# Batch 0 of an attention and SwiGLU kernel: running sums in 72-column segments, the causal mask by a product, single PSUM banks, and a new order of loads

## The chip, the cores and the metric

The kernel runs on one core of a Trainium2 chip. The time is the device time of one execution in microseconds (us). Every kernel was run several times, an experiment always beside runs of the kernel before on the same chip. The engines are called by the profile's names: PE (TensorE), DVE (VectorE), ACT (ScalarE), POOL (GpSimd), SP (SyncE); PEld is PE's weight load. The tiles in the profile's lines: rawk, rawq and rawv are the buffers in which loads land, ck and cq their bf16 casts, kq the transposed operands of the score product with the bias rows in them, HL and seg_rows the source of those rows, pt the exponentials, vt the cast V, ot the attention's output, XT its transpose, which the FFN reads, and wg, wv and wo the weights.

## The reference, cut to what matters

```python
# q, k, v: (8 batches, 8 heads, 576, 64)   s: (8, 8, 576)
cum = np.cumsum(np.maximum(s, 0.0), axis=-1)
bias = -(cum[:, :, :, None] - cum[:, :, None, :])
scores = np.where(causal, -1e9, q @ k.T / 8 + np.minimum(bias, 0.0))
attn = softmax(scores)                     # with the row maximum taken off
x = (attn @ v).transpose(0, 2, 1, 3).reshape(4608, 512)
g = x @ w_gate                             # w_gate, w_val: 512 x 1536
out = (g * sigmoid(g) * (x @ w_val)) @ w_out
```

The kernel brings the bias into the score product as extra rows of q and k: the running sum, split into a high and a low bf16 part, and constants.

## The kernel before

Batch 0's attention stands alone at the start. Then nine tiles of 512 tokens go through the feed-forward part (FFN), and the attention of the later batches is woven into them. The kernel fixes the order of each engine's instructions by the order of its Python calls. A "half batch" is four heads; half batches 0 and 1 are batch 0.

Loads of q, k and v go through SP's queue. There are three buffers for half batches, but one for V:

```python
def load_one(hb, name, rs=(0, NR)):          # "k" or "q" of one half batch
    ... loaded[name, hb] = raw.tile([...], tag="raw" + name)       # 3 buffers
    nc.sync.dma_start(...)
def load_v(b, cs):
    if 0 in cs:
        loaded["v", b] = raw.tile([...], tag="rawv", bufs=1)       # ONE buffer
    for c in cs:
        nc.sync.dma_start(t[0:n, c, :, :], v[b, ...])
```

The running sums, all 64 heads at once over 576 columns, then their rows by DMA into q and k:

```python
nc.vector.tensor_scalar(s_sb, s_sb, 0.0, 8.0, ALU.max, ALU.mult)
nc.vector.tensor_tensor_scan(c8, ones, s_sb, 0.0, ALU.mult, ALU.add)
nc.vector.tensor_copy(HL[:, 0, 1, :], c8)                           # high part
nc.vector.tensor_sub(HL[:, 1, 1, :], c8, HL[:, 0, 1, :])            # low part
nc.vector.tensor_copy(HL[:, 2:4, 0, :], HL[:, 0:2, 1, :])
```

Behind the last scores of batch 0 come the loads for what follows, and then the first FFN tile with "hooks" that run at given items (an item is roughly one gate or value product group):

```python
if h == 7:
    aug(3, SP4)                      # bias rows of half batch 3
    load_qk(3)
    load_v(1, range(5))
    load_qk(4)
    cast_one(2, "k", nc.gpsimd); cast_one(2, "q", nc.gpsimd)
    load_qk(5)
    w_load("o", 0); w_load("o", 1)
...
hook = {1: prep_one(2, 0), 2: prep_one(2, 1), 3: prep_one(2, 2), 4: prep_one(2, 3),
        6: cast_one(3, "k"), cast_one(3, "q")}                      # shortened
n0 = 6 if tt == 0 else 0             # item at which attention starts in the first tile
```

The load of V for batch 2 is not in this list. It is called from inside the attention code, when the third and fourth head of half batch 2 are scored.

The softmax here doesn't subtract the row's maximum and nothing guards it: scores larger than these inputs give would overflow.

## Time and profile before

| | kernel before |
|---|---|
| time, median of 3 runs | 381.24 us (380.64 to 382.00) |
| profiled span | 377.7 us |
| PE busy | 359.2 us, 95% of the span |
| first score product | 11.23 us |
| first gate product | 31.60 us |
| first gate product of the second tile | 79.38 us |
| last product | 373.29 us |

The prediction below shows most lines of this profile. Two views are added here, because they also belong here. The first is the order of work on SP from 50 to 66 us (start, length, queue, source line, what, count):

```profile
51.77 0.62 SPq L155 DMA_DIRECT2D rawk<-in_k_dram  x1
52.43 0.47 SPq L155 DMA_DIRECT2D rawq<-in_q_dram  x1
52.99 0.41 SPq L155 DMA_DIRECT2D rawk<-in_k_dram  x1
53.51 0.55 SPq L155 DMA_DIRECT2D rawq<-in_q_dram  x1
55.28 8.52 SPq L172 DMA_DIRECT2D rawv<-in_v_dram  x5
```

These are half batch 4, half batch 5, and then V of batch 2, in this order. (Before them, the five issues of V for batch 1 had held SP from 27.46 to 51.72 us, single ones for up to 7.31 us: half batches 4 and 5 stood behind V here too, but were still in time for their casts.) The second is one line of the order of work on ACT: the cast of half batch 5's k, with no idle time before it (a wait would stand in brackets at the end).

```profile
59.18 1.15 ACT L254 CAST ck<-rawk 128x1152 bf16<-128x1152 f32 x1
```

### The profile page before, as it was taken

What the parts mean: (1) busy time and instruction counts of PE and PEld (TensorE: products, weight loads), DVE (VectorE), ACT (ScalarE), POOL (GpSimd) and SP (SyncE); (2) the same over time, 40 slices, a digit from 0 to 9 for tenths busy, and PEclk for the clock granted to TensorE, in tenths of its full rate; (3) what the DMA queues carried; (4) which work ended last, traced back from release to release, by engine and by line L of the source; (5) the groups of instructions that cost most, each with busy time, mean ns of one, the idle gap of its engine ahead of it and who ended that gap; (6) DMA issues with size and microseconds to landing.
All of it is one profiled execution on the core that took longest, in us unless ns stands there. A gap on an engine that the chain in (4) does not pass through costs nothing.

```text
span 377.7 us, 8635 instructions
## 1 busy us (share of the span) xinstructions
PE 359.2 (95%) x3207; PEld 229.4 (61%) x3246; DVE 289.9 (77%) x577; ACT 242.7 (64%) x459; POOL 207.7 (55%) x326
## 2 busy tenths in 40 slices
PE   3679999999999999999999999999999999999996
PEld 3566556655555556865586558655875575466465
DVE  7766787457895899769975998589958876975984
ACT  8686788677976877578766875697365523323321
POOL 7784357445374646595559556875675426214320
PEclk9899999999999999999999999999999999999999
DMA  7999999988487998499659765998223133001103
GB/s 243 198 250 263 198 254 272 343 252 177 162 179 247 232 282 219 104 252 309 160 163 286 197 161 164 238 189 162 51 74 109 26 26 128 0 2 69 43 2 111
DMA packets 100729, 64.22 MB, mean 170 GB/s; under 512 B 81888, under 2 KB 85824, under 8 KB 100688
## 3 DMA queue, kind: packets, MB, share of 16 engines
q1 hardware_dynamic: 91248, 46.15, 51.5%
q0 software_dynamic: 9440, 17.53, 18.2%
q8 instruction: 25, 0.41, 0.5%
q14 instruction: 16, 0.13, 0.1%
HBM read 37.90 MB, written 19.86 MB: 153 GB/s over the span
## 4 chain that ended last, share of the span: by engine, by line
PE 85%; DVE 6%; DMA 5%; ACT 2%; issue 1%; DVEq 0%; ACTq 0%; SPq 0%
PE bank L626 22%; PE bank L641 22%; PE bank L711 17%; PE bank L375 9%; PE bank L413 6%; PE bank L670 5%; DMA pk<-ks 2%; PE wide L375 2%; DVE pp L633 1%; ACT pt L388 1%; DVE kq L326 1%; DVE ht L649 1%; PE one L413 1%; DMA kq<-HL 1%; DMA s_sb<-in_s_dram 1%
## 5 line engine op out<-in xcount | busy, mean ns | idle before, releaser
L388 ACT ACTIVATE pt<-bank 128x512 bf16<-128x512 f32 x224 | 106.7, 506 | 26.2 <-PE bank L375 17.9
L626 PE MATMUL bank<-XT,wg 128*128 128x512 bf16 x420 | 109.7, 379 | 1.2 <-DVE pp L633 0.2
L641 PE MATMUL bank<-XT,wv 128*128 128x512 bf16 x411 | 109.3, 379 | 1.1
L631 ACT ACTIVATE th<-bank 128x512 bf16<-128x512 f32 x108 | 64.7, 599 | 58.8 <-PE bank L626 53.5
L633 DVE SCALAR_TENSOR_TENSOR pp<-th,bank 128x512 bf16<-128x512 bf16 x108 | 73.7, 683 | 23.8 <-ACT th L631 23.2
L649 DVE SCALAR_TENSOR_TENSOR ht<-pp,bank 128x512 bf16<-128x512 bf16 x108 | 74.1, 687 | 10.4
L658 POOL TENSOR_TENSOR ht<-ht 128x512 bf16<-128x512 bf16 x35 | 40.5, 1156 | 52.9 <-DVE su L656 52.8
L375 PE MATMUL bank<-kq 128*128 128x128 bf16 (+4 forms) x504 | 67.5, 240 | 0.3 <-DVE ht L649 0.2
L375 PEld LDWEIGHTS <-kq 128*128 128x128 bf16 x576 | 46.2, 98 | 33.8 <-issue 5.1
L641 PEld LDWEIGHTS <-wv 128*128 128x128 bf16 x432 | 38.3, 98 | 35.3
L626 PEld LDWEIGHTS <-wg 128*128 128x128 bf16 x432 | 38.4, 98 | 35.0 <-issue 1.1
L391 POOL TENSOR_SCALAR_AFFINE_SELECT pt<-pt 128x512 bf16<-128x512 bf16 x64 | 41.5, 648 | 30.9 <-ACT pt L388 30.4
L413 PEld LDWEIGHTS <-pt 128*128 128x128 bf16 x960 | 41.0, 98 | 16.6 <-issue 0.7
L413 PE MATMUL bank<-vt,pt 128*128 128x65 bf16 x840 | 41.8, 194 | 0.5 <-DVE ot L430 0.5
L447 POOL DMA_DIRECT2D xs<-ot x24 | 21.8, 908 | 28.0 <-DVE ot L430 28.0
L711 PEld LDWEIGHTS <-ht 128*128 128x128 bf16 x336 | 31.2, 98 | 4.3
L197 POOL DMA_DIRECT2D kq<-HL x52 | 32.7, 632 | 0.1
L430 DVE TENSOR_TENSOR ot<-bank,rc 128x320 bf16<-128x320 f32 x56 | 27.5, 492 | 1.9
L396 POOL TENSOR_SCALAR_AFFINE_SELECT pt<-pt 128x64 bf16<-128x64 bf16 x64 | 17.4, 272 | 18.5 <-ACT pt L388 18.3
L711 PEld LDWEIGHTS <-su 128*128 128x128 bf16 x252 | 23.6, 98 | 3.3
L670 PE MATMUL bank<-wo,ht 128*128 128x512 bf16 x90 | 24.2, 379 | 0.3
L776 POOL TENSOR_TENSOR ysb<-ysb 128x512 f32<-128x512 f32 x12 | 15.3, 1272 | 15.3 <-DVE ysb L770 15.3
(96 smaller groups left out, 395.6 us busy)
## 6 DMA issues: line engine op xcount, KB each, us to landing
rawk<-in_k_dram SPq DMA_DIRECT2D x15, 576.0 KB
rawq<-in_q_dram SPq DMA_DIRECT2D x15, 576.0 KB
rawv<-in_v_dram SPq DMA_DIRECT2D x32, 256.0 KB
out_dram<-ysb POOLq DMA_DIRECT2D x32, 256.0 KB, 3.8
xs<-ot POOLq DMA_DIRECT2D x24, 160.0 KB, 4.0
ks<-ck SPq DMA_DIRECT2D x11, 288.0 KB
qs<-cq SPq DMA_DIRECT2D x11, 288.0 KB
wg<-in_moe_w_gate_dram POOLq DMA_DIRECT2D x2, 768.0 KB, 11.8
```

What stands on the lines that cost most here:

```text
L375: nc.tensor.matmul(sc[:, o : o + w], T[:, 1, e * S + 128 * tj : e * S + 128 * (tj + 1)], T[:, 0, e * S + lo : e * S + hi], start=True, sto ...
L388: nc.scalar.activation(pt[:, c0 : c0 + W], sc[:, 0:W], AF.Exp, scale=0.125)
L391: nc.gpsimd.affine_select(pt[:, 1088:1600], pt[:, 1088:1600], pattern=[[0, 4], [1, 128]], compare_op=ALU.is_ge, fill=zreg, base=0, channel ...
L413: nc.tensor.matmul(av[:, bi * (D + 1) : (bi + 1) * (D + 1)], pt[:, c0 : c0 + 128], VT[b % 2][:, tj, h, :], start=(tj == 0), stop=(tj == bi),)
L626: nc.tensor.matmul(pg, WG[j][:, c, f0 : f0 + 128], xt[:, c, :], start=(c == 0), stop=(c == 3),)
L631: nc.scalar.activation(th, pg, AF.Tanh, scale=0.5)
L633: nc.vector.scalar_tensor_tensor(pp, in0=th, scalar=1.0, in1=pg, op0=ALU.add, op1=ALU.mult)
L641: nc.tensor.matmul(pv, WV[j][:, c, f0 : f0 + 128], xt[:, c, :], start=(c == 0), stop=(c == 3),)
L649: nc.vector.scalar_tensor_tensor(hp[:, 2 * k2 : 2 * k2 + 2, :].rearrange("p a n -> p (a n)"), in0=pp, scalar=0.5, in1=pv, op0=ALU.mult, op ...
L658: (nc.vector if ft == NFT - 1 else nc.gpsimd).tensor_sub(hp[:, 1:3, :], hp[:, 1:4:2, :], hp[:, 0:3:2, :])
L670: nc.tensor.matmul(py, hps[ft // 2][:, 2 * (ft % 2) + half, c0 : c0 + 128], WO[ft // WKO][:, ft % WKO, :], start=(ft == 0), stop=(ft == NF ...
L711: nc.tensor.matmul(ps, lhs(p), rhs(p), start=(first and p == 0), stop=(last and p == NP - 1), skip_group_check=True,)
```

## The change

Its intent is to start the scores of batch 0 earlier, keep PE and ACT busier until the FFN begins, and spread the loads. Core of the diff, with cuts:

```diff
+    seg_c, seg_s, seg_tri, seg_rows, lower = ...        # small tiles; pt buffers 8 -> 7
-    2 two-bank tiles and 4 one-bank tiles in PSUM, regrouped after batch 0
+    8 one-bank tiles throughout
 # running sums of batch 0 on (8 heads x 8 segments) x 72
+    nc.vector.tensor_scalar(seg_s, ...); nc.vector.tensor_tensor_scan(seg_c, ...)
+    nc.tensor.matmul(bank[0:64, 0:1], seg_tri, seg_c[:, SEG - 1 : SEG])   # sums of earlier segments
+    nc.vector.tensor_add(seg_s, seg_c, bank...); high and low part into seg_rows
+    aug_first(0, 0)                                     # 4 row DMAs on SP; 12 more later
     nc.vector: maximum, scan and high part of the other batches (576 columns), now behind these
 # mask (batch 0 only)
-    POOL affine_select on the exponentials
+    matmul(sc, ident, lower, start=True, stop=False)    # adds -32768 above the diagonal
 # queues
-    load_qk(1) at the very start; V, half batches 2 and 3 on SP
+    load_qk(1) on SP behind aug_first(0, 0); V(0), weights, half batches 2 and 3 on POOL's queue
 # end of batch 0
+    values(0, 1) behind scores(5), values(2, 3) behind scores(6), the rest behind scores(7)
+    six gate products of 2 column blocks on the 3 head pairs that are ready, ahead of the last transposes
 # first FFN tile
-    the lists shown above; n0 = 6; prep of half batch 3 at steps (0,3) (1,3) (2,1) (2,3)
+    at_item(4 and 5, cast_one, 2, ...); at_item(5, init_vt, 1); at_item(6, load_v, 1)
+    at_item(6 to 9, prep_one, 2, ...); at_item(14, cast_one, 3, ...)
+    at_item(14, w_load, "o", 0); at_item(15, load_qk, 4); at_item(16, w_load, "o", 1)
+    at_item(20, load_qk, 5)
+    n0 = 10; prep of half batch 3 at steps (1,3) (2,1) (2,3) (3,1)
```

## The prediction

> **What bounds the kernel now.** I read the page first (engine shares, then the 40 slices), then the busy time by stretches, then the chain of waits of the first 36 us, then the order of work on each engine up to 60 us. The page says PE is busy for 359.2 of 377.7 us, so the question is only where the missing 18.5 us lie. The stretches (columns: start and end, length, busy time and count of PE, PEld, DVE, ACT, POOL, then granted clock, DMA share, GB/s) answer it:
>
> ```profile
> 12.00:13.00 1.00, 0.14 (x3) 0.04 (x1) 0.64 (x1) 1.00 (x2) 0.09 (x2) 0.90 0.71 164
> 14.00:15.00 1.00, 1.00 (x11) 0.96 (x10) 0.00 (x0) 1.00 (x2) 0.00 (x0) 0.50 1.28 229
> 22.00:23.00 1.00, 0.28 (x3) 0.18 (x2) 0.00 (x0) 1.00 (x2) 1.00 (x3) 1.00 1.17 223
> 28.00:29.00 1.00, 1.00 (x29) 0.86 (x27) 0.82 (x4) 0.72 (x2) 1.00 (x2) 1.00 1.17 214
> ...
> 31.60:40.00 8.40, 8.29 (x56) 4.59 (x59) 6.34 (x9) 5.66 (x10) 2.30 (x2) 1.00 1.13 253
> 40.00:50.00 10.00, 9.43 (x71) 5.38 (x71) 7.84 (x13) 8.80 (x19) 2.39 (x5) 1.00 1.21 199
> 160.00:200.00 40.00, 39.79 (x379) 26.56 (x382) 31.82 (x68) 29.43 (x59) 26.74 (x41) 1.00 0.89 222
> ```
>
> Until 11 us PE waits for data, from 12 to 23 us it idles behind ACT, from 23 us it is full. From 31.6 us (the first gate product) to 377.7 us it is busy 339.3 of 346.1 us, and of the 6.8 us missing 3.75 lie after 320 us. So nearly all that this change can win lies before 31.6 us, and nothing in it shortens the 346 us after that. The chain of waits (start, length, what) shows what sets the 31.6 us:
>
> ```profile
> 0.81 2.93 DMA s_sb<-in_s_dram
> ...
> 4.35 1.36 DVE c L237
> ...
> 7.94 3.24 DMA kq<-HL
> ...
> 11.88 1.03 ACT pt L388
> ...
> 14.44 1.91 PE one L297 x18
> ...
> 24.00 0.92 PE one L413 x30
> 24.91 0.80 PE wide L375 x9
> 25.71 1.36 PE one L413 x45
> ...
> 30.91 0.65 ACT XT L468
> 31.56 0.04 issue
> 31.60 0.38 PE bank L626
> ```
>
> Three pieces: s, its scan and split, and the bias rows' DMA, up to 11.2 us; sixteen exponentials that end at 26.96 us; then values, transposes and a wait for the last copy into XT, 4.64 us more. ACT runs one head in 1.675 us once steady, from the order of work on ACT:
>
> ```profile
> 20.26 6.70 ACT L388 ACTIVATE pt<-wide 128x1024 bf16<-128x1024 f32 x8
> ```
>
> 13.3 us for eight heads, plus the two gaps ACT has before it (0.56 us at 14.0 and 1.27 us at 16.83), is the 15.1 us of this stage.
>
> **What the Trainium skill says.** "ScalarE: Activation LUTs", What ACT_TABLE_LOAD costs: an ACTIVATE with immediates takes 186 ns + 0.833 ns a column, back-to-back ones overlap by about 93 ns. That gives 1039 ns for 1024 columns; this trace has 1024. Splitting a head's two exponentials into four should then cost some 0.1 to 0.2 us a head; the trace, where later heads already run as four, has four of them in 1.69 us, so almost nothing. "TensorE: Matmul & The Clock Gate", Part 1: an idle PE drops to half clock and needs about 3.4 us of work to come back. The trace agrees: clock 0.50 from 13 to 16 us after the wait at 10 to 11, and the 18 transposes there take 1.91 us, 106 ns each; later ones take some 72 ns (five in 0.36 us). "VectorE: DVE Perf Modes", Zero memsets can be issued as uint32: a memset takes one cycle per element whatever its type. The trace is a little better, 1.07 us for 1216 columns, so about 0.56 us for 608. "DMA: Bandwidth & Descriptors", Issuing engines are not separate DMA queues: moving loads to another queue only saves issue time, the engines are shared. The DMA share of 1.0 to 1.3 from 13 us on agrees that order, not queue, matters.
>
> **The change part by part.**
>
> Running sums by segments. The scan over 576 columns (1.35 us), the casts (0.83, 0.75, 0.45 us) leave the head of the chain. In their place, on 64x72: maximum, scan, a one-column product over the segments, add, cast, difference. I estimate 0.25, 0.25, 0.45, 0.25, 0.15, 0.2 us and 0.2 for handovers, from the 0.19 us of the 128x5 reciprocal and an eighth of the long ones: 1.75 us. DVE first has four new memsets of 608 columns, 4 x 0.59 from 1.0 us, to 3.4 us; s lands at about 3.6; the rows are ready at about 5.4 us instead of 7.85. Four row DMAs at 0.62 to 0.83 us of issue, the last landing 2.2 us later (the shortest of this kind): 10.0 us instead of 11.18. Taken alone that is 1.2 us won.
>
> But scores(0) also needs q's columns, which DVE copies from PSUM, and DVE's program order now has in front of them: the long maximum 0.55, the long scan 1.37, the HL cast 0.84 (for later batches), and three memsets 1.77 us. 5.4 + 4.53 = 9.9; two copies 1.5 (the trace has 1.44 and 1.46 a pair): 11.4 us. So the first product moves from 11.2 to about 11.4, the first exponential stays near 11.9. The wait on the row DMA becomes a wait on DVE.
>
> DVE stays behind: cast of q's second half 0.45, k's copies 1.5 and q's 1.5 (k's moved from ACT), cast of k of the second half batch 0.78: 15.7 us. PE's order puts that batch's k transposes before scores(2), so scores(2) starts at about 16.4 and ACT, done with two heads at 11.9 + 3.4 = 15.3, waits about 1.4 us. Before, ACT waited 0.56 + 1.27 = 1.83 us. Nothing won.
>
> Mask by a product. Per head it adds a 512- and a 64-column product to PE, 0.22 + 0.03 us (a 512-column product of the gate advances 0.86/4 = 0.215 us): 2.0 us for eight heads, and removes 0.63 + 0.24 us of POOL. The first five are free, since PE idles 0.76 to 0.86 us a head there; the last three cost up to 0.75 us, because from 23 us PE is full. The POOL selects were off the chain.
>
> Single banks. Four exponentials a head, 1.69 against 1.675 us: 0.1 us over eight heads. Gain: PE no longer waits for a two-bank tile, but seven banks less four held by transposes leave three, so it runs little ahead. I call it zero.
>
> Values earlier, gates on three pairs. After scores(5) values 0 and 1 (0.55 us a head: 15 products in 0.55 to 0.57), after scores(6) 2 and 3, after scores(7) the rest. With ACT at the end of head 5 at 11.9 + 6 x 1.69 + 1.6 = 23.6, PE ends scores(5) at some 22.2; values 1.1, scores(6) 1.05, values 1.1, scores(7) 1.05: 26.5; values 4, 5 1.1; transposes and values 6 (0.37 + 0.55 + 0.74), values 7 0.55: 29.8; six gate products 1.3 in the place of 14 warming products: 31.1; last transposes 0.4 and copy 0.7: 32.2. At that moment 1.3 us of the FFN is done, so the comparable start is 30.9 us against 31.6.
>
> Loads. V, weights and the next batches go by POOL's queue. In the kernel before, 17.2 us pass from 12.5 us (end of the quiet spell) to 29.7 us (value weights issued at 16.67 landed 13.0 us later), for V, two weight blocks and one half batch. The same sum of bytes now starts near 8.5 us, so they land near 26 to 27 us, before their use at 31. Hidden. In the first FFN tile attention starts four items later; ACT was busy 8.8 of 10 us at 40 to 50 and stays off the chain; of the 0.57 us PE lost there perhaps 0.3 is won.
>
> Sum: 0.7 + 0.3 = 1.0 us by this working, 380.2 us.
>
> **The rivals.** (1) DVE is quicker than I add up, and the rows' DMA decides after all: scores from 10.0 us, no wait at head 2. Then the whole stage is 1.4 + 1.4 us earlier and the gain is 3 to 4 us: 377 to 378. For it: the change is plainly aimed at this, and it fills PE with warming products to be ready; my small-operation times are estimates. Against: the DVE sum is made of measured durations. (2) Loads starve the FFN: V on POOL's queue costs POOL perhaps 1 us an issue (0.91 us for the 24 stores of ot), a gate block lands 10.0 to 13.7 us after issue here, so one that leaves at 15 to 18 us may land after 30 us. That would take back 1 to 3 us: 381 to 383. Against: POOL is freed of selects, and the DMA has 4 us more. (3) Bias rows of heads 2 to 7 come too late: twelve more small DMAs on SP in line behind q and k, 0.62 us each, landing 2.2 to 7.0 us later in this trace. Heads 2 and 4 have 1 us of slack or less, so 0 to 2 us lost.
>
> **Range and chances.** The working gives 380.2. The estimates that could move it mostly err towards a gain (rival 1, and PE at full clock in the transposes), so I take about 1 us more: 379.3 us. Low end, rival 1 in full and some of the first tile's gaps: 376.2. High end, rival 2 or 3 cancelling the tail's gain: 381.6. Faster by over 2% needs 373.6 us, 7.6 us less: the stage before 31.6 us would have to shrink by a quarter, chance 0.04. Slower by over 2% would need starving of 7.6 us, 0.02.
>
> **What would show each step.** Right: first score product at about 11.4 us with DVE's copy of q, not DMA, as its releaser; a gap on ACT of more than 1 us before head 2; four exponentials in 1.69 us; last exponential at 27 to 28 us; gate products among the last values; the first value product at about 32 us; clock near 1.0 from 10 us on. Wrong: scores at 10 us released by the row DMA (rival 1); PE waiting for a DMA of wg or wv around 30 us (rival 2) or of kq rows at scores(2) or (4) (rival 3); a PE below 97% after 32 us would show a cost in the first tile that I left out.

## The result, and the profile after

| | before | after |
|---|---|---|
| time, median of 4 runs | 380.94 us (379.87 to 382.00) | 391.56 us (391.11 to 393.02) |
| profiled span | 377.7 us | 388.6 us |
| mean granted clock | 0.995 | 0.991 |
| first score product | 11.23 us | 11.52 us |
| first gate product of the second tile | 79.38 us | 89.47 us |
| last product | 373.29 us | 383.82 us |

The changed kernel is slower: ratio 1.0285, 95% interval 1.0245 to 1.0326. Here and below a ratio is the mean time of one kernel's fast runs over that of the other's of the same rounds, so it is not quite the ratio of the medians.

The table of milestones splits the loss. At the second tile the changed kernel is 10.09 us behind, at the last product 10.53. So nearly all of it arises before 90 us. For the end of batch 0 the two kernels must be compared with care, since the changed one does six gate products early. Its seventh (the chunk that waits for the last transpose) starts at 33.87 us; six products at 0.215 us are 1.3 us, so its comparable start is 32.58 us against 31.60. Batch 0 lost about 1.0 us, and the first FFN tile about 9.1.

The stretches that answer to those in the prediction, for batch 0 (start and end, length, busy time of PE, PEld, DVE, ACT, POOL, granted clock, DMA share, GB/s):

```profile
12.00:13.00 1.00, 0.34 (x4) 0.16 (x3) 0.97 (x3) 1.00 (x3) 1.00 (x2) 1.00 1.05 404
14.00:15.00 1.00, 0.90 (x11) 0.63 (x9) 1.00 (x2) 0.56 (x2) 0.35 (x2) 1.00 1.03 229
22.00:23.00 1.00, 1.00 (x12) 0.76 (x12) 1.00 (x3) 0.92 (x4) 1.00 (x3) 1.00 1.18 208
```

The clock is 1.00 where it was 0.90 and 0.50, and PE is full at 22 us where it was busy 0.28: the intent came true there in this execution. For the clock that is partly chance: with the same batch 0, e1 has 3.41 us at half clock from 13.28 us and e2 from 18.87, and of the seven runs of the kernel before in their round four have a mean clock of 1.000. The chain of waits of the same kernel shows what it met (start, length, what):

```profile
11.13 0.63 SPq L200
11.81 6.59 DMA kq<-seg_rows
18.53 0.40 PE bank L419 x4
...
33.18 0.65 ACT XT L511
33.87 4.04 PE bank L673 x18
```

The bias rows of heads 2 and 3 leave SP behind half batch 1's 1.15 MB and land at 18.4 us. ACT sat idle 2.82 us before head 2, where the kernel before had two gaps of 0.56 and 1.27.

Now the first tile. PE's waits after 32 us, in the changed kernel (engine, tile and line, what it waited for: total us, times, longest):

```profile
PE bank L419 <- ACT pt L429: 3.3, 1, 3.3
PE bank L419 <- DVE kq L376: 2.2, 2, 1.4
PE bank L673 <- ACT XT L511: 0.7, 1, 0.7
```

In the kernel before, the same view has no wait above 0.5 us. The 3.3 us wait is for an exponential, but ACT was not slow: it was waiting itself. Its order of work, and SP's:

```profile
63.90 0.60 ACT L429 ACTIVATE pt<-bank 128x512 bf16<-128x512 f32 x1 [0.43 <-PE bank L419]
70.17 1.15 ACT L304 CAST ck<-rawk 128x1152 bf16<-128x1152 f32 x1 [5.67 <-DMA rawk<-in_k_dram]
71.22 0.70 ACT L429 ACTIVATE pt<-bank 128x512 bf16<-128x512 f32 x2
```

```profile
44.61 0.56 SPq L148 DMA_DIRECT2D rawk<-in_k_dram  x1
45.21 0.47 SPq L148 DMA_DIRECT2D rawq<-in_q_dram  x1
59.40 5.54 SPq L165 DMA_DIRECT2D rawv<-in_v_dram  x5
64.98 0.62 SPq L148 DMA_DIRECT2D rawk<-in_k_dram  x1
```

Read SP's lines against those of before. Half batch 4 leaves at 44.61 us. Then SP issues nothing for almost 14 us, because the next instruction in its order is V of batch 2, which needs the only V buffer, which POOL is casting V of batch 1 out of until 59.37 us. Half batch 5, called at item 20, now stands behind it: it leaves at 64.98 us in place of 52.99, and lands at 70.09. ACT reaches its cast at 64.5 us, waits 5.67 us for it, and cannot do the exponentials behind it. The Trainium skill states both halves of this. "DMA: Bandwidth & Descriptors", section "Anatomy of one DMA — SWDGE (gpsimd) path", says that a semaphore wait of a DMA happens on the issuing sequencer before dispatch; "PSUM — Partial Sum Buffer", section "Engine vs sequencer instructions", says that ScalarE's queue is strictly first in, first out. Both agree with these lines: almost 14 us without an issue on SP, with a load behind the waiting one, and 5.67 us on ACT with exponentials behind the cast.

What the wait costs PE, from the busy times in single microseconds (columns as above):

```profile
70.00:71.00 1.00, 0.00 (x0) 0.00 (x0) 0.00 (x0) 0.83 (x1) 0.00 (x0) 1.00 1.03 403
72.00:73.00 1.00, 0.99 (x7) 0.63 (x6) 0.00 (x0) 0.99 (x2) 0.24 (x1) 0.50 1.04 401
76.00:77.00 1.00, 1.00 (x14) 0.74 (x12) 0.17 (x1) 1.00 (x3) 0.24 (x1) 0.50 0.15 60
```

PE stands still for 3.29 us to 71.87, and then works at clock 0.50 until 77.86 us. It is busy for 5.6 of these 6.0 us, so by my estimate half of that, about 2.8 us, is lost as well. The half clock itself lasts from 71.03 to 77.86 us, 6.83 us. Followed in windows of 0.1 us from 3 to 370 us, each of the 16 profiles here has one or two such stretches, and each of them lasts 3.41 us (the kernel before, from 12.80) or two or three times as long (10.24 us in e12 below, from 66.69). So what a wait costs also depends on where it falls: in e3, where ACT waits about as long for the same load, the half clock in the tile lasts only 3.41 us, from 70.52. The rest of the tile's loss is short waits: 1.40 and 0.83 us for DVE's copies into kq, 0.7 to 0.8 us more for POOL and ACT; together some 9 us with the two large ones. That is a sum of readings. The experiments test it.

### The profile page after: what moved, and what is told of

It reads as the page before. It is cut to its first block, busy times and chain, and to the rows that moved or that the text cites.

```text
span 388.6 us, 8828 instructions
## 1 busy us (share of the span) xinstructions
PE 368.7 (95%) x3288; PEld 232.9 (60%) x3288; DVE 293.7 (76%) x585; ACT 242.1 (62%) x472; POOL 213.3 (55%) x328
## 4 chain that ended last, share of the span: by engine, by line
PE 80%; DVE 6%; ACT 3%; DMA 3%; SPq 3%; issue 3%; POOL 1%; DVEq 0%; ACTq 0%; POOLq 0%
PE bank L673 41%; PE bank L762 16%; PE bank L419 9%; PE bank L456 7%; PE bank L721 5%; DMA kq<-seg_rows 2%; ACT pt L429 2%; SPq L165 1%; DMA rawk<-in_k_dram 1%; DVE kq L376 1%; SPq L200 1%; DVE pp L689 1%; DVE ht L700 1%; ACT kq L374 1%; PE bank L506 1%
## 5 line engine op out<-in xcount | busy, mean ns | idle before, releaser
L429 ACT ACTIVATE pt<-bank 128x512 bf16<-128x512 f32 (+1 forms) x256 | 120.4, 508 | 35.4 <-PE bank L419 25.2
L673 PE MATMUL bank<-XT,wv 128*128 128x512 bf16 x432 | 110.8, 379 | 0.2 <-DVE ht L700 0.2
L419 PE MATMUL bank<-kq 128*128 128x128 bf16 (+4 forms) x576 | 76.0, 241 | 8.0 <-DVE kq L376 3.5
L434 POOL TENSOR_SCALAR_AFFINE_SELECT pt<-pt 128x512 bf16<-128x512 bf16 x56 | 37.1, 663 | 40.4 <-ACT pt L429 28.1
L456 PEld LDWEIGHTS <-pt 128*128 128x128 bf16 x960 | 41.2, 98 | 16.7 <-issue 1.1
L456 PE MATMUL bank<-vt,pt 128*128 128x65 bf16 x960 | 46.4, 194 | 0.6 <-DVE ot L473 0.5
L473 DVE TENSOR_TENSOR ot<-bank,rc 128x320 bf16<-128x320 f32 x64 | 31.4, 491 | 2.4 <-DVE rc L472 0.2
L191 POOL DMA_DIRECT2D kq<-HL x48 | 29.5, 616 | 0.1
L721 PE MATMUL bank<-wo,ht 128*128 128x512 bf16 x96 | 25.9, 394 | 0.0
L439 POOL TENSOR_SCALAR_AFFINE_SELECT pt<-pt 128x64 bf16<-128x64 bf16 x56 | 15.8, 282 | 18.3 <-ACT pt L429 18.2
L376 DVE COPY kq<-bank 64x640 bf16<-64x640 bf16 (+1 forms) x26 | 19.3, 766 | 7.1 <-PE bank L347 6.8
```

Of the source, the lines that this page charges most:

```text
L419: nc.tensor.matmul(sc[:, o : o + w], T[:, 1, e * S + 128 * tj : e * S + 128 * (tj + 1)], T[:, 0, e * S + lo : e * S + hi], start=not maske ...
L429: nc.scalar.activation(pt[:, c0 : c0 + n], sc, AF.Exp, scale=0.125)
L434: nc.gpsimd.affine_select(pt[:, 1088:1600], pt[:, 1088:1600], pattern=[[0, 4], [1, 128]], compare_op=ALU.is_ge, fill=zreg, base=0, channel ...
L456: nc.tensor.matmul(av[:, bi * (D + 1) : (bi + 1) * (D + 1)], pt[:, c0 : c0 + 128], VT[b % 2][:, tj, h, :], start=(tj == 0), stop=(tj == bi),)
L473: nc.vector.tensor_mul(ot[:, :, e * D : (e + 1) * D], av3[:, :, 0:D], rc[:, :, None].to_broadcast([128, NCH, D]),)
L673: nc.tensor.matmul(view(bs, TT), w[:, c, f0 : f0 + 128], xt[:, c, :], start=(c == 0), stop=(c == 3),)
```

## The experiments

Theory A, from the traces: the loss is the new order of the first tile, above all that the load of half batch 5 fell behind V of batch 2 on SP. Its rivals: the loss comes from batch 0 (its loads, rows or engine order), with the tile only passing it on; or the tile suffers from its later casts and the attention that starts four items later. "Excess" below is a kernel's median less that of the kernel before of the same rounds; for the changed kernel it is 10.6 us. Three rounds each.

### e1: half batch 5 loaded right behind half batch 4

```diff
 at_item(15, load_qk, 4)
+at_item(15, load_qk, 5)
-at_item(20, load_qk, 5)
```

> The changed kernel with one line moved: q and k of half batch 5 are issued at item 15 of the first FFN tile, behind those of half batch 4, in place of item 20. Theory A (the load stands on SP behind the second V load, which waits for V's buffer; ScalarE then waits 5.7 us for it in order, PE idles 3.3 us and runs 6.6 us at half clock): the wait goes, the time falls by 5.5 to 7 us, to 384.5 to 386. Rival (the DMA engines have too much to do by then, so the data come late whenever they are asked for): under 2 us, 389.5 or more.

Measured: 385.11 us, ratio 1.0138 (1.0111 to 1.0165), excess 4.9. Theory A holds: one load moved by five items brings back 5.7 of 10.6 us. The second tile's first gate products start at about 83 us where they started at 89.47.

### e2: new batch 0, the first tile's old order

```diff
 scores(7)
 aug(3, SP4)
+load_v(1); load_qk(4); cast_one(2, "k"); cast_one(2, "q"); init_vt(1); load_qk(5); w_load("o", 0 and 1)
-all at_item(...) lines; n0 = 10; the new prep steps
+the hooks, n0 = 6 and prep steps of the kernel before
```

> The changed kernel's batch 0 with the kernel before's order of the first FFN tile: V of batch 1, q and k of half batches 4 and 5 and the output weights issued at the end of batch 0, half batch 2 prepared at items 1 to 4, attention from item 6. Theory A (about 9 of the 10.1 us lost up to the second tile come from the first tile's order, 1 from batch 0): 381 to 383. Rival (batch 0's new load order leaves the DMA queues late, and the first tile only shows it): 386 to 391.

Measured: 383.46 us, ratio 1.0087 (1.0066 to 1.0108), excess 3.2. A little over A's range, far under the rival's. Batch 0 costs about 3 us when the tile behind it is the old one, more than the 1.0 us that I read off the milestones. The clock accounts for most of the first part of that: head 2's scores start at 18.64 us, in the changed kernel at 18.53, then PE runs at half clock until 22.28 us here, and the seventh gate product starts at 34.72 in place of 33.87.

### e3: old batch 0, the first tile's new order

The reverse of e2, from the kernel before.

```diff
-the loads, casts and output weights behind scores 7; the hooks; n0 = 6; the old prep steps
+the at_item(...) lines of the changed kernel, n0 = 10, its prep steps
```

> The kernel before's batch 0 with the changed kernel's order of the first FFN tile; nothing else of the change. Theory A: 389 to 391, nearly the whole loss without segments, mask product, single banks or gate products. Rival (the loss needs batch 0's new queues): 381 to 384.

Measured: 387.40 us, ratio 1.0198 (1.0167 to 1.0228), excess 7.2. It lies between the two ranges. The tile's order alone does most of the damage, with ACT's cast waiting 5.24 us for the load; and 3.2 + 7.2 = 10.4 is close to the whole change's 10.6, so within their intervals (about 1 us each way) the two parts add.

### e4: bias rows of heads 2 and 3 ahead of half batch 1's load

```diff
-load_qk(1)
 aug_first(0, 1)
+load_qk(1)
```

> The changed kernel with the bias rows of heads 2 and 3 issued on SP ahead of q and k of half batch 1. In the trace the last of these rows lands at 18.4 us and head 2's scores start at 18.53; the transposes of half batch 1 free them at about 17.3. Theory (rows held behind 1.15 MB in SP's queue): scores of head 2 start about 1.1 us earlier, released by PE or DVE and not a DMA, 0.5 to 1.2 us off the total, 390.4 to 391. Rival (half batch 1 then lands as much later and its cast sets head 2 instead): no change within 0.3 us.

Measured: 395.65 us, ratio 1.0399 (1.0369 to 1.0429). Both missed; its excess is 15.4 us, 4.8 more than that of the changed kernel. The rows no longer wait, but half batch 1 does: PE waits 3.54 us for DVE's cast of its k, which waits for the load, and 1.74 for POOL's cast of its q. Two needs of the same moment stand in one queue, and this order is the worse one.

### e5: half batch 1's load back at the start

```diff
 load_one(0, "q", (r, r + 1))
+load_qk(1)
 ...
-load_qk(1)
 aug_first(0, 1)
```

> The changed kernel with q and k of half batch 1 issued where the kernel before has them, at about 3.5 us, ahead of the first bias rows and of V. Theory B (in batch 0 these two loads are the urgent ones: asked for at 8.3 us and sharing the engines with V, they hold up the cast on VectorE, the transposes ahead of head 2's scores and the rows behind them in SP's queue): head 2's scores start near 17.0 us, not 18.5, and the total falls by 1 to 2.5 us, to 389 to 390.5. Rival (1.15 MB ahead of the first bias rows keeps them from landing before 11.5 us): the first scores start at 12 us or later, released by the DMA of the rows, and nothing is won: 391 to 393.

Measured: 390.12 us, ratio 1.0255 (1.0229 to 1.0282). The total is in range by the one theory, the mechanism is the rival's. PE's waits of this kernel:

```profile
PE bank L420 <- DMA kq<-seg_rows: 3.1, 1, 3.1
```

The first bias rows now stand behind 1.15 MB, the first scores start at 13.56 us and not at 11.52, and the clock is at half until 18.7 us. That what head 2 gains pays for it is my reading and was not tested.

### e6: e2 and e5 together

```diff
 load_one(0, "q", (r, r + 1))
+load_qk(1)                        # the first tile as in e2
```

> The old order of the first tile (383.5 with the rest of the change) and the early q and k of half batch 1 together. Theory B: 1 to 2.5 us less than that, 381 to 382.5, about the time of the kernel before. Rival (batch 0 loses its 3.2 us to the mask product and the values' order on a full PE): 383 to 384.

Measured: 382.50 us (six runs), ratio 1.0067 (1.0043 to 1.0090), excess 2.4. The gate product that waits for the last transpose starts at 32.90 us, 1.8 us earlier than in e2, but only some 0.8 us of that reaches the end, and this is not clear of noise, as the intervals of e2 and e6 overlap. The total is at the upper end of theory B's range. Up to there the program is that of e5, and yet the first scores start at 12.22 us here and at 13.56 there: one profile of each is too little to tell differences of 1 us at this place.

### e7: e6 with less of DVE ahead of the first scores

The long running-sum chain for later batches moved behind half batch 1's copies, three memsets moved from DVE to POOL.

```diff
-tensor_scalar, tensor_tensor_scan, tensor_copy of the 576 columns; aug_consts(1, 1, nc.vector)
 load_v(0, range(5), nc.gpsimd)
+aug_consts(1, 1, nc.gpsimd)
 ...
 pe_out(1, nm, g, 1, nc.vector)
+tensor_scalar, tensor_tensor_scan, tensor_copy of the 576 columns
```

> As the run before, and VectorE freed ahead of q's first copies: the long running sum and its cast go behind half batch 1's copies, the three memsets for half batch 1 to GpSimd behind the V loads. Theory (VectorE's order set the first scores at 11.5 us, 4.4 us of work that is not needed yet): the first scores start at 10.0 to 10.5 us, released by the DMA of the bias rows or by VectorE's copies; 0.5 to 1.5 us off the run before, 380 to 381.5. Rival (head 2 is set by half batch 1's cast and transposes, which end no earlier): first scores earlier, total within 0.4 us of the run before.

Measured: 388.34 us, ratio 1.0198 (1.0153 to 1.0242): missed by 7 us. DVE's copies of q were done at 9.88 us and not at 11.5, but the scores waited for the rows until 13.46. And the late chain held POOL, which needs its result, and behind POOL the weight loads and half batch 3: issued at 31.0 to 33.2 us instead of 25.0 to 27.2. PE then waited 2.65 us for POOL's cast. By this trace it is the same fault as in the first tile, on another queue; what share of the 5.8 us over e6 it makes up was not tested.

### e8: the changed kernel without the six early gate products

```diff
-for ft in range(2):
-    products("g", ft, XT[:, :, 0:TT], range(3))
```

> The changed kernel without the six gate products ahead of the last transposes; they run when their tile begins. If they fill time in which PE would wait for the last copy into XT, as the prediction has it: PE waits some 2 us there, the total rises by 0.8 to 1.3 us, to 392.4 to 392.9. Rival (what follows is bound elsewhere, by the bias rows and loads of the first tile): no change within 0.4 us.

Measured: 390.93 us, ratio 1.0283 (1.0260 to 1.0306). The total is the changed kernel's within 0.3 us of excess, as the rival says. But that doesn't show that the six products win nothing. Without them PE idles 1.08 us before the last transposes, and the same point of the work, the third group of gate products, starts at 36.85 us in place of 36.02: 0.83 us later, which is what the theory expected. The first tile then gives it back, and the second tile starts at 89.53 us in place of 89.47: in e8's profile the half clock lasts 3.41 us, in the changed kernel's 6.83. The mean clocks of all runs agree, 0.991 to 0.996 against 0.985 to 0.991. So the end of the kernel doesn't decide between theory and rival.

### e9: e2 with half batch 1's load on POOL's queue at 4.4 us

```diff
+for nm in ("k", "q"):
+    load_one(1, nm, eng=nc.gpsimd)      # in POOL's gap, ahead of aug_first(0, 0)
 ...
-load_qk(1)
 aug_first(0, 1)
```

> Old first-tile order (as in e2) with the load of the second half batch put on GpSimd's queue at about 4.4 us, in GpSimd's own gap, so that on SP's queue nothing but the first 1.2 MB lies ahead of the bias rows. Theory (the rows of a queue land in the queue's order; e5 to e7 lost the head because 1.15 MB stood ahead of them): first scores at 11.4 to 11.7 released by DVE's copy, as in the changed kernel, no half clock at 13 to 18 us, and no wait of heads 2 and 3 for their rows, because those now leave SP right behind the first: 380.5 to 381.8 us, 0.7 to 2 us under e6 (382.5). Rival (the engines, not the queue, hold the rows: 1.15 MB more in flight slows them in any queue): first scores at 12 or later, total 382 to 383.5.

Measured: 381.81 us (13 runs), ratio 1.0061 (1.0037 to 1.0085), excess 1.9. As e6 within the intervals. First scores at 11.84 us: between the two expectations. PE's weight load names the rows:

```profile
PEld L421 <- DMA kq<-seg_rows: 1.5, 1, 1.5
```

The DMA engines are almost full until 9.7 us here, while in the changed kernel they fall quiet from 7.3 to 9.5, and PE's first weight load with rows in it runs at 10.17 us there and at 11.81 here. So in this trace a queue of its own did not bring 2.2 KB rows past 1.15 MB. It cost the first scores little, since DVE's copy of q ended at 11.65 us. This is the best version with the new batch 0, and still not better than the kernel before.

### e10: e9 with the long chain at 19 us, and POOL's use of it behind POOL's loads

```diff
 half_batch("q")
+tensor_scalar, tensor_tensor_scan, tensor_copy of the 576 columns    # from ahead of scores(0)
 scores(3)
 ...
-other_rows()
 w_load("g", 1); w_load("v", 1); load_one(3, "k" and "q")
+other_rows()                      # and aug_consts(1, 1) on POOL, as in e7
```

> e9 with the long running-sum chain moved behind half batch 1's query copies (about 19 us instead of 5.8 to 8.2), three memsets of 0.6 us moved to GpSimd behind V's loads, and GpSimd's use of the chain moved behind its loads, which e7 had left waiting. Theory (DVE's program order, as the prediction said, is what holds the first scores once the rows are there): first scores at 10.0 to 10.6, released by the rows' DMA or by DVE, total 379.3 to 380.7, about 1 us under e9. Rival (the head isn't what sets the end of batch 0, values and the last copy into XT are): head earlier, but total within 0.4 us of e9.

Measured: 388.45 us, ratio 1.0217 (1.0175 to 1.0258): missed. First scores at 12.05 us although q was copied at 9.88. What held them is not settled: the profile names a DVE copy that ends at 12.02 but goes into the tile of heads 2 and 3, and by its view of seg_rows PE's first weight load waited 1.3 us for the rows. The chain then stood in DVE's order ahead of copies that the later heads need (PE waited 3.9 us in all for DVE's copies into kq, 0.8 of it at the first scores), and one cast beside POOL's work took very long:

```profile
14.86 2.74 DVE L302 CAST ck<-rawk 128x1152 bf16<-128x1152 f32 x1
```

The same cast takes 0.76 us in the kernel before. PE waited 3.1 us for it.

### e11: e9 with POOL's selects for heads 4 to 7

```diff
-masked = bh < H
+masked = bh < HB
```

> e9 with the mask product kept for heads 0 to 3 only; heads 4 to 7 have GpSimd's two selects again. Theory (PE is full from 24 us, so the four heads' products, 4 x 0.25 us, lie on the path): 0.6 to 1.0 us under e9. Rival (GpSimd, full from 14 to 31 us, pays 4 x 0.87 us for it, and values wait for the selects or the loads behind them go out later): same as e9 or up to 2 us over it.

Measured: 386.28 us, ratio 1.0162 (1.0124 to 1.0201). The rival holds, and more:

```profile
PE bank L458 <- POOL pt L436: 2.7, 1, 2.7
```

The selects stand behind six load issues and four other operations in POOL's order and start at 28.20 us. The mask product, 0.25 us of PE a head, buys freedom from that order.

### e12: the kernel before with half batch 5's load moved behind V of batch 2

```diff
-load_qk(5)                       # behind scores(7)
+20: [lambda: load_qk(5)]         # a hook of the first tile
```

> The kernel before with one thing moved: the load of half batch 5 comes behind V of batch 2 in SP's program order instead of ahead of it (both instructions otherwise the same, all other engines the same). Theory (the loss of the change is this one inversion: V's load waits for the single V buffer and holds the next load behind it): rawk of half batch 5 issued at about 64 us instead of 53, landing at about 69; ACT's cast of it waits some 5 us, PE idles about 3 us near 70 us and then runs at half clock for some 4 us: 384.5 to 387 us, 4 to 6 us lost. Rival (the inversion only bites together with the rest of the new first-tile order, its later casts and its attention that starts four items later): 380 to 382 us.

Measured: 391.11 us, ratio 1.0274 (1.0197 to 1.0351), excess 11.1: one load moved in the kernel before costs as much as the whole change. ACT and SP of this kernel:

```profile
60.83 0.62 SPq L155 DMA_DIRECT2D rawk<-in_k_dram  x1
62.00 0.47 SPq L155 DMA_DIRECT2D rawk<-in_k_dram  x1
```

```profile
68.94 1.15 ACT L254 CAST ck<-rawk 128x1152 bf16<-128x1152 f32 x1 [9.68 <-DMA rawk<-in_k_dram]
```

The loss was twice what I expected, and the trace shows two reasons. I had not seen that in this position the load also comes behind half batch 6, which takes the place at 60.83 us. And the old tile reaches ACT's cast at 59.3 us, 5.2 us earlier than the new one, so ACT waits longer. PE stood still for 8.7 us to 71.36, and the clock was at half from 66.7 to 76.9 us.

### e13: the same, but directly behind V and ahead of half batch 6

```diff
 load_v(bn, (2, 3, 4))            # in the attention code, V of batch 2 for bn == 2
+if bn == 2:
+    load_qk(5)
 ...
-load_qk(5)                       # behind scores(7)
```

> The kernel before with the load of half batch 5 moved directly behind V of batch 2 in SP's program order, and still ahead of half batch 6 (in e12 it had come behind half batch 6 too). Theory (the wait of V for its buffer, then V's own bytes, hold the load): issued at about 61 us, 1.2 us earlier than in e12, and with 1.2 MB less ahead of it, landing at 65 to 67 us; ACT's cast waits 6 to 7.5 us instead of 9.7; 386 to 389 us. Rival (most of e12's loss came from half batch 6 in front of it): 382 to 384 us.

Measured: 387.78 us, ratio 1.0206 (1.0179 to 1.0233), excess 7.9, by the theory:

```profile
66.26 1.15 ACT L254 CAST ck<-rawk 128x1152 bf16<-128x1152 f32 x1 [6.72 <-DMA rawk<-in_k_dram]
```

The load leaves at 61.27 us. The inversion with V alone, with nothing else new in the kernel, costs 7.9 us; half batch 6 in front of it some 3 more. Of the delay itself the wait for the buffer is the smaller part here: half batch 4's issues end at 52.77 us, V's first starts at 55.50, and its five issues take until 61.23. In the changed kernel the wait was 13.7 us and the issues took 5.54. No run gave V a second buffer, so what the buffer alone costs is not shown; the place behind V is.

### e14: e1 with the old order of casts, transposes and attention, the new order of loads

```diff
-at_item(4 and 5, cast_one, 2); at_item(6 + i, prep_one, 2, i); at_item(14, cast_one, 3); n0 = 10
+casts of half batch 2 behind scores(7); at_item(1 + i, prep_one, 2, i); at_item(6, cast_one, 3); n0 = 6
```

> e1 with the order of work in the first tile put back on every engine but SP's and GpSimd's load queues: casts of half batch 2 behind scores 7, transposes at items 1 to 4, casts of half batch 3 at item 6, attention from item 6; V of batch 1, half batches 4 and 5 and the output weights stay where the changed kernel has them, with half batch 5 early as in e1. Theory C (the rest of the loss is attention starting four items later and its transposes in the way of copies): 383 to 384 us, as e2. Rival (it is the place of the loads, V of batch 1 and output weights six items in): 384.8 to 386 us, as e1.

Measured: 391.67 us, ratio 1.0310 (1.0275 to 1.0345): both missed. SP's order of work says why:

```profile
33.12 25.46 SPq L165 DMA_DIRECT2D rawv<-in_v_dram  x7
58.68 4.90 SPq L148 DMA_DIRECT2D rawk<-in_k_dram  x1
```

Attention starts four items earlier, so its call of V for batch 2 comes ahead of item 15, and now half batches 4 and 5 both stand behind it: five transfers of V for batch 1, the first two of V for batch 2, and only then half batch 4, at 58.68 us (e1: 44.80). PE waits 6.7 us for POOL's casts, ACT 8.55 us. What costs the 1.7 us between e1 and e2 is therefore not separated; but the same inversion has shown itself a third time, by an edit that touched no load.

## Why the prediction was wrong, point by point

What it got right. The first scores start at 11.52 us, released by DVE's copy of q (predicted 11.4, the same releaser). A head's four exponentials take 1.69 us. The clock is 1.00 from 12 us until the stall in the first tile, though only in the profiled execution, as e1 and e2 show. The six gate products do run between the last values and the last transposes. The 11.4 is in part luck: by DVE's order of work the rows were ready at 5.91 us (predicted 5.4), the work behind them took 4.20 us (4.53) and the two copies 1.36 (1.5), so the errors cancel.

What it mis-sized in batch 0. ACT's gap before head 2 was to be 1.4 us and is 2.82: DVE's cast of half batch 1 took 1.62 us and not 0.78, and the rows came at 18.4 us; rival 3 had the second with "0 to 2 us lost". The last exponential ends at 29.56 us, predicted 27 to 28. The six early gate products were to win 1.3 us in place of warming products; e8 shows some 0.8 us at their place, and none at the end of the kernel. The first value product starts at 34.08 us, predicted 32. One reading of the profile before was wrong as well: from 12 to 23 us PE doesn't just idle behind ACT, it is busy for 7.03 of the 11 us, 3.25 of them at half clock. So "0.7 us won" became about 1 us lost in the profile, and 3.2 us in the times of e2. Part of that is the chance of the clock, and part is still unexplained: in e6 and e9 the start of the FFN is level with the kernel before (32.90 and 32.99 us less 1.3), and some 2 us remain at the end.

Where it failed. The step is the last sentences of "Loads": "In the first FFN tile attention starts four items later; ACT was busy 8.8 of 10 us at 40 to 50 and stays off the chain; of the 0.57 us PE lost there perhaps 0.3 is won." I took the busy share of ACT as the test of whether the tile could suffer, and asked of the moved loads only whether they reach their use in batch 0. I did not write down SP's order of instructions before and after. It was there to be read: V of batch 2 is called by the attention code, half batch 5 at item 20, and V waits for one buffer. In the tile 9.1 us were lost; e1, e12 and e13 show the cause of the larger part by moving that one load, in both kernels: 5.7 us come back in e1, and 7.9 are lost in e13. Of the rest, the short waits, e1 still has 2.2 us for DVE's copies; no run separates them. The prediction named the sign ("a PE below 97% after 32 us would show a cost in the first tile that I left out"), and from 31.6 to 80 us PE is busy 41.2 of 48.4 us, 85%, but it gave this no place in the range: slower by over 2% had a chance of 0.02. Rival 2 looked for starved loads as well, but of weights and at 30 us.

The size of the loss also has a part that no sum of waits shows: after 3.29 us of idling PE ran at half clock for 6.0 us. The prediction used that effect at the start of the kernel, as a gain, and not as what multiplies any new wait.

## What to carry to other kernels

When a change moves loads, list each queue's instructions in program order before and after, and mark those that wait for a buffer: everything behind a waiting load waits with it, however early it is called, and behind its issues as well, which for the five of V took over 5 us here. A load whose call comes from another piece of code (here attention) can change places with yours when either moves, so look at the order that comes out and not at the item number. And an engine with 10% of slack over a stretch is no protection against one late input.

## What the Trainium skill lacked or had wrong

- "DMA: Bandwidth & Descriptors", "Anatomy of one DMA — SWDGE (gpsimd) path", says where a DMA's semaphore wait happens, but not what follows for the loads behind it in the same program. Here it follows: half batch 5's load left at 64.98 us in place of 52.99, ACT waited 5.67 us; the same inversion alone in the kernel before cost 7.9 us.
- "DMA: Bandwidth & Descriptors", "Issuing engines are not separate DMA queues", is right, but gives no figure for how small transfers fare beside large ones: PE's first weight load with the 2.2 KB rows in it ran at 10.17 us with the 1.15 MB load behind them (changed kernel), at 12.19 to 13.53 with it ahead in the same queue (e5 to e7), and at 11.81 with it in another queue (e9).
- "SBUF — State Buffer", "Who interferes with whom", gives the rule that DVE's casts and POOL's work share ports, but no size for this pair: the 128x1152 cast took 0.76 us in the kernel before, 1.62 beside POOL's cast and memsets in the changed one, 2.74 beside them and a load's issue in e10. That POOL is the cause was not tested.
- "TensorE: Matmul & The Clock Gate", Part 1, calls its window of about 3.4 us free-running and has the clock return after a busy one, which agrees with half-clock stretches of 3.41, 6.83 and 10.24 us. But it has the clock fall after an idle window, and doesn't say how idle: in the 3.41 us before the fall PE was still busy for 1.37 us in the kernel before (9.39 to 12.80) and for 0.96 us in the changed one (67.62 to 71.03).
